# Longer landing times and queue holds for four kinds of loads in a kernel's own instruction planner: pooled attention and a gated MLP, fp32

## The chip, the cores and the metric

The kernel runs on one core of one Trainium2 chip. The metric is the device time of one execution in microseconds (us), lower is better. The engines are TensorE (PE; PEld is its weight load), VectorE (DVE), ScalarE (ACT), GpSimd (POOL), and the queue of SyncE (SP), which issues nearly all DMAs.

## The reference

Attention over pooled keys and values, then an MLP with a GELU of sigmoid form over all 4608 tokens (8 batches of 576), in fp32:

```python
q, k, v: (8, 8, 576, 64)                     # batch, heads, sequence, head width
k_p, v_p = mean over 8 successive positions  # 72 pooled keys and values
attn = softmax(q @ k_p^T / 8) @ v_p
x = attn, heads side by side                 # (4608, 512)
h = x @ w_in                                 # 512 -> 2048
out = (h * sigmoid(1.702 h)) @ w_out         # 2048 -> 512
```

## The kernel before

**The work.** Every fp32 product is made of three products of split operands (a rounded part and the rest): high by high, high by low, low by high. Batches 0 and 1 go through the MLP in the plain way (`dense`, L1208 to L1210 and L1250 to L1252). From batch 2 on the first product of the MLP is made in pairs of hidden blocks by a scheme with seven block products in place of eight (`pair`, products on L1412 into two banks of PSUM that the profile names `ha` and `hb`). It needs sums of blocks of the weights, which `fold` forms once (`stage`, L1295 to L1323), stores to DRAM (`wd`), and which `fetch_pair` loads again for each chunk (`ws` and `shared`, L1345, 512 and 256 KB each). A chunk is 512 tokens of one batch; its eight pairs follow each other on PE, with the second MLP product (`o`, L1613 to L1615) of the pair before between them. A ninth chunk takes the 64 tokens left over in each batch.

**The attention of batch b runs under the MLP of the batches before it.** For b from 2 on its steps are these. The keys come in two loads (`kv_False`, u = 0 and 1), the values in two (`kv_True`), the last eight pooled positions in two (`tl`), each by `fetch_main` and `fetch_tail` on SP; q comes in eight loads (`qr`, two pieces of the sequence by four pairs of heads), each of four DMAs, by `fetch_q`. There is one buffer for `kv` loads after the first batch, one for `tl` and two for `qr`, so a load also waits for the reader of the one before it. DVE sums the eight positions of each pool (`red_k` and `red_v`, L544, about 2 us; `tred`, L605, about 1 us), spreads the sums over block diagonals (`kbd`, `vbd`, L554; `tbd`, L615), and transposes q (`qt`, L731). PE transposes the keys (`kps`), makes the scores (`sps`, L747); DVE and ACT make the softmax (`nm`, `sc`, `sm`), PE the weighted values (`pav`, L949 to L952). What comes out is split and combined for the seven-product scheme (`combine`, L1013 and L1019, tiles `x`, `xs`, `xt`).

**Inside a pair** PE writes seven products into `ha` and `hb`. Between two products into `ha`, `keep` must have copied the bank to SBUF (L1427, ACT or DVE). `plus` (L1434, DVE) adds `hb` to what was kept. ACT then makes the GELU twice (L1451, L1459), POOL or DVE the low part (L1466), and the result feeds the `o` products of the next pair's time. ACT and DVE each take their instructions strictly in the order of the list. A `plus` that comes late therefore holds ACT at the GELU, and a `keep` that stands behind it on ACT holds PE.

**The order of everything** is a list that the kernel works out before it emits a single instruction (class `Plan`). Each step is a task with an engine, an estimated duration and a due time; `order` runs the tasks in a model and emits them in the order in which the model started them. A DMA occupies one modelled queue for its bytes over a rate (340 GB/s for long runs, 80 GB/s for the 128-byte runs of q), and its reader becomes ready 2.2 us after that (`wait`, L126 to L136). So in the list before the change a reader stands no earlier than this after the last DMA of its load began: keys and values 262,144 B / 340 GB/s + 2.2 = 2.97 us; `tl` 65,536 B / 340 GB/s + 2.2 = 2.39 us; q 32,768 B / 80 GB/s + 2.2 = 2.61 us. A table of hand-set shifts of due times (`SHIFTS`) names steps of batches 0 to 2 for the most part; its entries are the same before and after. Nothing in the list changes at run time: each engine executes its part in order and waits on semaphores where the data is not there.

Of the kernel before, what the change touches and what calls it, by code (L numbers as in the profile page):

```python
# [26 lines left out]
WARM = 222.0  # L27
SLACK = 1.5
BLOCKED = 20.0

# [33 lines left out]


class Task:
    __slots__ = "engine us emit due after before bufs ready left begun table k port other mode kind".split()


class Plan:
# [3 lines left out]
    def __init__(self):  # L76
        self.tasks, self.due, self.start = [], 0.0, 0.0

    def add(self, engine, us, emit, reads=(), writes=(), due=None, table=None, also=(), port=False, other=None, mode=None):


        t = Task()
        t.engine, t.us, t.emit, t.table, t.port, t.other = engine, us, emit, table, port, other
        t.due = self.due if due is None else due
        t.mode = mode
        names = [(b[0] if isinstance(b, tuple) else b).name for b in (*writes, *reads)]
        what, number = re.match("([a-z]*)(.*)", names[0]).groups()
        if what in ("raw", "e", "w"):
            number = ""
        else:  # L90
            halves = [n for name in names for n in re.findall("[0-9]_[0-9]+", name)]
            number = (halves or [number])[0]
        t.kind = f"{engine} {what}{number}"
        t.k = len(self.tasks)
        t.before, t.after = set(), []
        t.bufs = []
        for group, is_write in ((reads, False), (writes, True)):
            for b in group:
                b, key = b if isinstance(b, tuple) else (b, None)
                if b not in t.bufs:  # L100
                    t.bufs.append(b)
                    b.users += 1
                for other, k2 in b.writes + (b.reads if is_write else []):
                    if (key is None or k2 is None or key == k2) and not (
                        is_write and engine == other.engine == "DMA" and (other, k2) in b.writes
                    ):
                        t.before.add(other)
                (b.writes if is_write else b.reads).append((t, key))
        for b in also:
            if b not in t.bufs:  # L110
                t.bufs.append(b)
                b.users += 1
        t.before.discard(t)
        for o in t.before:
            o.after.append(t)
        t.left, t.ready, t.begun = len(t.before), self.start, None
        self.tasks.append(t)
        return t
# [8 lines left out]
    @staticmethod  # L127
    def wait(a, b):

        if a.engine == b.engine and a.engine != "DMA":  # L130
            return 0.0
        if a.engine == "DMA" or b.engine == "OUT":
            return 2.2
        if b.engine == "PE":
            return 0.25 if b.due < 150 else 1.2
        return 0.2  # L136
# [15 lines left out]
    def order(self):  # L152
# [33 lines left out]
        while len(placed) < len(self.tasks) or running:  # L186
# [13 lines left out]
            for e in ENGINES:  # L200
# [5 lines left out]
                for t in ready[e]:  # L206
                    if t.ready > now + 1e-9 or e != t.engine and now < t.due:
                        continue
                    rank = (t.due + (BLOCKED if blocked and t.port and e == "DVE" else 0.0), t.k)
                    if (best is None or rank < best[0]) and self.room(t, wanted):  # L210
# [46 lines left out]
def attention_moe_kernel(ctx: ExitStack, tc: tile.TileContext, q, k, v, w_in, w_out, out):  # L257
# [41 lines left out]
    plan = Plan()  # L299
    rings = {}  # L300

    def buf(pool, shape, dtype, tag, name, bufs=None, fifo=False):
        n = bufs or {"xpool": 2, "moe": 2, "ps_o": 4, "ps_h": 2, "ps_a": 2}.get(pool.name, 1)
        ring = rings.setdefault((pool.name, tag), Ring(n, fifo))
        kw = {"bufs": bufs} if bufs else {}
        return Buf(ring, lambda: pool.tile(shape, dtype, tag=tag, name=name, **kw), name)

    def dma(nbytes, emit, reads=(), writes=(), due=None, run=2048):

        us = nbytes / 1e3 / (340.0 if run >= 1024 else 190.0 if run >= 256 else 80.0)  # L310
        return plan.add("DMA", us, emit, reads, writes, due)

    def act(n, emit, reads, writes, table=None, due=None):
        return plan.add("ACT", 0.17 + n * 0.85e-3, emit, reads, writes, due, table)
# [128 lines left out]
    class Part:  # L443
# [8 lines left out]
        @property  # L452
        def ref(self):
            return (self.of, self.key)
# [4 lines left out]
    def fetch_main(b, u, src, t=None):  # L459

        if t is None:
            t = buf(load, [P, NP, 512], F32, "kv", f"kv{b}_{u}_{src is v}", fifo=True)
        for a in range(2):
            dma(
                KM * NP * 2048,
                lambda a=a: nc.sync.dma_start(
                    out=t()[a * KM : (a + 1) * KM],
                    in_=src[b, UH * u + a : UH * (u + 1) : 2, 0 : KM * POOL].rearrange(
                        "j (p w) d -> p j (w d)", w=POOL
                    ),  # L470
                ),
                writes=[ref(t)],
            )
        return t

    def fetch_tail(b, u):

        tl = buf(load, [P, 512], F32, "tl", f"tl{b}_{u}", fifo=True)
        for r, src in enumerate((v, v, v, k)):
            dma(  # L480
                TAIL * 2048,
                lambda r=r, src=src: nc.sync.dma_start(
                    out=tl()[r * TAIL : (r + 1) * TAIL],
                    in_=src[b, UH * u : UH * (u + 1), KM * POOL :].rearrange("h (p w) d -> h p (w d)", w=POOL),
                ),
                writes=[ref(tl)],
            )
        return tl

    def fetch_last(b, part=None):  # L490

        tl = part or buf(load, [P, 512], F32, "tl", f"tl{b}", fifo=True)
        for r, src in enumerate((v, k)):
            dma(
                KM * 2048,
                lambda r=r, src=src: nc.sync.dma_start(
                    out=tl()[r * KM : (r + 1) * KM].rearrange("p (h d) -> p h d", h=H),
                    in_=src[b, :, KM * POOL :].rearrange("h s d -> s h d"),
                ),
                writes=[ref(tl)],  # L500
                run=256,
            )
        return tl

    def fetch_q(b, piece, j):

        o0, tiles = PIECES[piece]
        npc = sum(m for _, m in tiles)
        qr = buf(load, [P, PMAX // 32, 32], F32, "qr", f"qr{b}_{piece}_{j}", bufs=2, fifo=True)
        for a in range(2):  # L510
            for e in range(2):
                r = (2 * a + e) * 32
                dma(
                    32 * npc * 4,
                    lambda r=r, a=a, e=e: nc.sync.dma_start(
                        out=qr()[r : r + 32, 0 : npc // 32],
                        in_=q[b, 2 * j + a, o0 : o0 + npc, e * 32 : (e + 1) * 32].rearrange("(c i) d -> i c d", i=32),
                    ),
                    writes=[qr],
                    run=128,  # L520
                )
        return qr

# [44 lines left out]
    def sum_keys(b, m):  # L568
# [3 lines left out]
        if b < TURNED:  # L572
            tl = m.tl or fetch_last(b)
        for u in range(NU):
            raw = m.k[u] if m.k else fetch_main(b, u, k)
            if b >= TURNED:
                tl = fetch_tail(b, u)
# [87 lines left out]
    def sum_values(b, m):  # L665
        m.vbd = buf(att, [P, NJ, 2, D], F32, "bd", f"vbd{b}", fifo=True)
        for u in range(NU):
            raw = m.v[u] if m.v else fetch_main(b, u, v)
            spread(b, raw, m.vbd, u, f"v{u}")
# [32 lines left out]
    def scores(b, piece, m, whole_q=None):  # L702
# [9 lines left out]
        for j in range(NJ):  # L712
            qt = buf(att, [P, PMAX], F32, "qt", f"qt{n}_{j}", bufs=2)
            if whole_q:
                qps = buf(ps_o, [P, DM], F32, "o", f"qps{n}_{j}")

                def turn(j=j, qps=qps):
                    for (s0, ns), src in zip(tiles, whole_q):
                        nc.tensor.transpose(
                            qps()[:, s0 - o0 : s0 - o0 + ns],  # L720
                            src()[:, 2 * j : 2 * j + 2].rearrange("p h d -> p (h d)"),
                            ident[:ns, :ns],
                        )

                pe(112 * len(tiles), turn, [ref(s) for s in whole_q], [qps], also=[qt])
                copy(npc, lambda copy, qt=qt, qps=qps: copy(out=qt()[:, :npc], in_=qps()[:, :npc]), [qps], [qt])
            else:
                qr = fetch_q(b, piece, j)
                dve(
                    npc,  # L730
                    lambda qt=qt, qr=qr: nc.vector.transpose(  # L731
                        qt()[:, :npc], qr().rearrange("p c d -> p (c d)")[:, :npc]
                    ),
                    [qr],
                    [qt],
                )
# [847 lines left out]
    def begins(c):  # L1584
        return FIRST + STEP * (NF + LAG) + ROUND * (c - 1)
# [41 lines left out]
    for c in range(FROM, B + 1):  # L1627
        acc = {}
        for p in range(NPAIR):
            due = begins(c) + ROUND * p / NPAIR  # L1630
# [45 lines left out]
```

## Time and profile before

| what | value |
|---|---|
| median of 3 runs | 944.16 us (943.03 to 945.93) |
| the profiled execution, its own time | 946.76 us |
| its span, first to last instruction | 944.9 us |
| PE busy in the span | 913.2 us (97%) |
| DVE, ACT, POOL busy | 661.0, 549.2, 311.5 us |
| mean granted TensorE clock | 0.994 |
| DMA moved | 176.71 MB, mean 187 GB/s |

The profile is of one execution, which took 1.86 us more than its span and 2.60 us more than the median of the runs. An engine's idle time is given with what ended it. PEclk is the granted TensorE clock as a share of full speed. A chain of waits goes back from the last instruction to what released each step. In the names, `tred<-tl` is the step that writes `tred` and reads `tl`; the numbers of batches and buffers are left out in the profile. In the rows of the instruction order further down they are kept: `tred7_1` belongs to batch 7, second half of the heads, and the last number only counts buffers.

### The profile page before, as it was taken

To read this page: it belongs to the slowest core of one execution; us is meant where nothing else is said; L and a number is where in the kernel's file an instruction comes from. 1 tells how busy PE (TensorE), PEld (TensorE's weight loads), DVE (VectorE), ACT (ScalarE), POOL (GpSimd) and SP (SyncE) were. 2 spreads that over 40 slices of the span, in tenths; PEclk is the share of its full clock that TensorE was granted. 3 is DMA by queue.
4 is the path that set the end of the run, shared out by engine and by line. 5 is a ranking of instruction groups with operands and counts; after the bars stand their busy time and mean duration, and the time that the engine had idled before them with its cause. 6 is when DMAs were issued, how large, how long until landed. Compare 5 with 4: busy or idle time off the path is not lost.

```text
span 944.9 us, 16303 instructions
## 1 busy us (share of the span) xinstructions
PE 913.2 (97%) x5689; PEld 814.7 (86%) x5689; DVE 661.0 (70%) x1236; ACT 549.2 (58%) x1218; POOL 311.5 (33%) x295
## 2 busy tenths in 40 slices
PE   9999999999899999999999999999899999999997
PEld 9888898888688989898789888988798999899986
DVE  5989878986787777888588867886688642223222
ACT  3778755444448665776467736774477564445443
POOL 1668731878233214225122432233122460000000
PEclk9999999999999999999999999999899999999999
DMA  9994423546647478845884588458764666557541
GB/s 255 376 373 126 122 68 102 155 127 222 187 116 209 135 202 232 235 139 172 250 235 143 182 226 254 152 156 241 213 191 145 206 194 209 164 176 230 178 136 45
DMA packets 145265, 176.71 MB, mean 187 GB/s; under 512 B 85664, under 2 KB 96928, under 8 KB 145184
## 3 DMA queue, kind: packets, MB, share of 16 engines
q1 hardware_dynamic: 140336, 166.89, 59.7%
q10 hardware_dynamic: 4848, 8.78, 2.6%
q8 instruction: 45, 0.74, 0.3%
q14 instruction: 36, 0.29, 0.1%
HBM read 150.47 MB, written 25.17 MB: 186 GB/s over the span
## 4 chain that ended last, share of the span: by engine, by line
PE 71%; DMA 12%; DVE 6%; SPq 6%; ACT 2%; issue 2%; POOL 0%; ACTq 0%; DVEq 0%; POOLq 0%
PE ha L1412 14%; PE hb L1412 11%; PE o L1615 9%; PE o L1614 9%; PE o L1613 9%; DMA qr<-in_q_dram 3%; DMA raw<-in_moe_w_out_dram 3%; PE sps L747 3%; PE h L1208 2%; PE h L1210 2%; PE h L1209 2%; PE o L1251 2%; PE o L1250 2%; PE o L1252 2%; DMA out_dram<-osb 2%
## 5 line engine op out<-in xcount | busy, mean ns | idle before, releaser
L1615 PE MATMUL o<-w,glall 128*128 128x512 f32 x448 | 176.7, 394 | 0.0
L1613 PE MATMUL o<-w,ghall 128*128 128x512 f32 x448 | 176.7, 394 | 0.0
L1614 PE MATMUL o<-w,ghall 128*128 128x512 f32 x448 | 176.1, 393 | 0.0
L1466 POOL TENSOR_TENSOR glall<-shared,ghall 128x256 fp32r<-128x256 f32 x84 | 71.0, 848 | 210.2 <-ACT shared L1459 160.9
L1412 PE MATMUL hb<-x,ws 128*128 128x256 f32 x672 | 99.6, 284 | 4.9 <-DVE shared L1434 3.6
L1412 PEld LDWEIGHTS hb<-x,ws 128*128 128x128 f32 x672 | 91.4, 189 | 13.5 <-DVE shared L1434 7.0
L1412 PEld LDWEIGHTS ha<-xs,ws 128*128 128x128 f32 x672 | 93.3, 189 | 8.4 <-DVE shared L1427 1.6
L1615 PEld LDWEIGHTS o<-w,glall 128*128 128x128 f32 x448 | 84.4, 188 | 18.5
L1412 PE MATMUL ha<-xs,ws 128*128 128x256 f32 x672 | 98.7, 283 | 0.7 <-DVE shared L1427 0.7
L1451 ACT ACTIVATE ghall<-shared 128x256 fp32r<-128x256 f32 x150 | 62.5, 417 | 54.9 <-DVE shared L1434 35.4
L1613 PEld LDWEIGHTS o<-w,ghall 128*128 128x128 f32 x448 | 84.8, 189 | 7.7
L1614 PEld LDWEIGHTS o<-w,ghall 128*128 128x128 f32 x448 | 84.3, 188 | 7.8
L1427 ACT COPY shared<-ha 128x256 f32<-128x256 f32 x116 | 43.0, 371 | 79.5 <-PE ha L1412 73.5
L1466 DVE TENSOR_TENSOR glall<-shared,ghall 128x256 fp32r<-128x256 f32 x66 | 33.1, 502 | 67.4 <-ACT shared L1459 64.9
L1466 POOL TENSOR_TENSOR glall<-gall,ghall 128x256 fp32r<-128x256 f32 x44 | 38.3, 874 | 107.1 <-ACT gall L1459 82.7
L1434 DVE TENSOR_TENSOR shared<-shared,hb 128x256 f32<-128x256 f32 x112 | 46.4, 414 | 38.5 <-PE hb L1412 29.7
L1459 ACT ACTIVATE shared<-shared 128x256 f32<-128x256 f32 x150 | 62.7, 418 | 4.8
L1208 PE MATMUL h<-x,w 128*128 128x256 f32 (+1 forms) x192 | 63.7, 332 | 0.0
L1209 PE MATMUL h<-x,w 128*128 128x256 f32 (+1 forms) x192 | 61.9, 322 | 0.3 <-DVE w L1143 0.3
L1210 PE MATMUL h<-x,w 128*128 128x256 f32 (+1 forms) x192 | 61.7, 321 | 0.0
L1412 PEld LDWEIGHTS ha<-x,shared 128*128 128x128 f32 x336 | 47.4, 191 | 12.6 <-ACT shared L1427 5.0
L1412 PE MATMUL ha<-x,shared 128*128 128x256 f32 x336 | 50.0, 285 | 6.4 <-ACT shared L1427 4.1
(175 smaller groups left out, 2099.9 us busy)
## 6 DMA issues: line engine op xcount, KB each, us to landing
ws<-wd SPq DMA_DIRECT2D x168, 512.0 KB
shared<-wd SPq DMA_DIRECT2D x56, 256.0 KB
out_dram<-osb ACTq DMA_DIRECT2D x32, 256.0 KB
wd<-stage SPq DMA_DIRECT2D x16, 512.0 KB
raw<-in_moe_w_in_dram SPq DMA_DIRECT2D x15, 512.0 KB
raw<-in_moe_w_out_dram SPq DMA_DIRECT2D x15, 512.0 KB
kv_False<-in_k_dram SPq DMA_DIRECT2D x28, 256.0 KB
kv_True<-in_v_dram SPq DMA_DIRECT2D x28, 256.0 KB
```

The costliest lines, as they stand in the source:

```text
L1208: nc.tensor.matmul(o, lhsT=w[:, 0, j], rhs=xs[:, 0], start=j == 0, stop=False)
L1209: nc.tensor.matmul(o, lhsT=w[:, 1, j], rhs=xs[:, 0], start=False, stop=False)
L1210: nc.tensor.matmul(o, lhsT=w[:, 0, j], rhs=xs[:, 1], start=False, stop=j == NJ - 1)
L1412: nc.tensor.matmul(o, lhsT=wv()[:, r, jj], rhs=xo(k, jj), start=start and n == 0, stop=n == len(terms) - 1,  skip_group_check=not start,)
L1427: t = copy(256, lambda copy: copy(out=part(i), in_=bank()[:, 0:256]), [bank], [at(i)])
L1434: lambda: nc.vector.tensor_tensor(out=part(i), in0=part(i), in1=hb()[:, half * 256 : half * 256 + 256], op=ALU.add),
L1451: lambda: nc.scalar.activation(out=gh(), in_=src(), func=AF.Gelu_apprx_sigmoid),
L1459: lambda: nc.scalar.activation(out=part(i), in_=src(), func=AF.Gelu_apprx_sigmoid),
L1466: engine.tensor_tensor(out=gl(), in0=part(i), in1=gh().bitcast(F32), op=ALU.subtract)
L1613: nc.tensor.matmul(o(), lhsT=gh()[:, tok], rhs=w()[:, 0], start=start, stop=False)
L1614: nc.tensor.matmul(o(), lhsT=gh()[:, tok], rhs=w()[:, 1], start=False, stop=False)
L1615: nc.tensor.matmul(o(), lhsT=gl()[:, tok], rhs=w()[:, 0], start=False, stop=stop)
```

## The change

Three kinds of load get a landing time of their own in the list (`LAGS`): keys and values 3.2 us in place of 2.2 (not in batch 0), `tl` 3.0, q 2.5. A DMA now also holds the modelled queue for at least 0.4 us, for `tl` at least 0.7 and for q at least 0.5. With both, the least distance from the start of the last DMA of a load to its reader becomes 0.77 + 3.2 = 3.97 us for keys and values, 0.7 + 3.0 = 3.7 us for `tl`, and 0.5 + 2.5 = 3.0 us for q. No step is added or removed and no operand changes; only the order changes, and for some copies and subtractions the choice between two engines.

```diff
+LAGS = {"kv": 3.2, "tl": 3.0, "qr": 2.5}
...
-    def add(self, engine, us, emit, reads=(), writes=(), due=None, table=None, also=(), port=False, other=None, mode=None):
+    def add(self, engine, us, emit, reads=(), writes=(), due=None, table=None, also=(), port=False, other=None, mode=None, lag=2.2):
...
-        t.mode = mode
+        t.mode, t.lag = mode, lag
...
-        if a.engine == "DMA" or b.engine == "OUT":
+        if a.engine == "DMA":
+            return a.lag
+        if b.engine == "OUT":
             return 2.2
...
-    def dma(nbytes, emit, reads=(), writes=(), due=None, run=2048):
+    def dma(nbytes, emit, reads=(), writes=(), due=None, run=2048, issue=0.4, lag=2.2):
-        us = nbytes / 1e3 / (340.0 if run >= 1024 else 190.0 if run >= 256 else 80.0)
-        return plan.add("DMA", us, emit, reads, writes, due)
+        us = max(issue, nbytes / 1e3 / (340.0 if run >= 1024 else 190.0 if run >= 256 else 80.0))
+        return plan.add("DMA", us, emit, reads, writes, due, lag=lag)
...
     def fetch_main(b, u, src, t=None):
+                lag=LAGS["kv"] if b else 2.2,
     def fetch_tail(b, u):
+                issue=0.7,
+                lag=LAGS["tl"],
     def fetch_q(b, piece, j):
+                    issue=0.5,
+                    lag=LAGS["qr"],
```

The order is the same up to the key sums of batch 1, and differs from there on. Three places matter below. Line numbers after the change are up to 9 higher than before (L1434 is L1443, L605 is L614, L466 is L470).

First place, DVE, before, while the chunk of batch 5 ends and the loads of batch 7 are read. `red7_k1` and `tred7_1` read the second keys and the second `tl` of batch 7; the rows with `hb5_6` and `hb5_7` are `plus` of chunk 5's last two pairs:

```order
L1466 TENSOR_TENSOR glall0_3104<-shared12_3020,ghall0_3096 128x256
L1434 TENSOR_TENSOR shared12_3020<-shared12_3020,hb5_6_7388 128x256
L544 TENSOR_REDUCE red7_k1_7509<-kv7_1_False_7459 128x128
L554 TENSOR_TENSOR kbd7_7453<-red7_k1_7509,mask2_84 128x256
L605 TENSOR_REDUCE tred7_1_7545<-tl7_1_7491 128x64
L1434 TENSOR_TENSOR gall_3155<-gall_3155,hb5_7_7512 128x256
L615 TENSOR_TENSOR tbd7_7479<-tred7_1_7545,mask4_86 128x256
```

The same place on DVE after the change:

```order
L553 TENSOR_REDUCE red7_k1_7453<-kv7_1_False_7384 128x128
L989 TENSOR_TENSOR xs6_3_7414<-pav6_1_3_7440,xs6_3_7414 128x256
L1443 TENSOR_TENSOR shared12_3019<-shared12_3019,hb5_6_7325 128x256
L563 TENSOR_TENSOR kbd7_7389<-red7_k1_7453,mask2_84 128x256
L1028 CAST xs6_2_7501<-xt6_1_7332 128x512
L1022 TENSOR_TENSOR xt6_0_6932<-xt6_0_6932,xt6_1_7332 128x512
L1443 TENSOR_TENSOR gall_3186<-gall_3186,hb5_7_7494 128x256
L1022 TENSOR_TENSOR xs6_4_7516<-xt6_1_7332,xs6_4_7516 128x512
L1475 TENSOR_TENSOR glall0_3140<-gall_3186,ghall0_3128 128x256
L1443 TENSOR_TENSOR shared12_3019<-shared12_3019,hb5_7_7494 128x256
L614 TENSOR_REDUCE tred7_1_7573<-tl7_1_7448 128x64
```

`tred7_1` stood two rows behind `red7_k1`, ahead of the first `plus` of pair 7; now it stands ten rows behind, after two of that pair's `plus`, with part of batch 6's combining between.

Second place, SP, before: the loads of batch 2's first keys, `tl` and q:

```order
L466 DMA kv2_0_False_1783<-in_k_dram 64x2x512 x2
L482 DMA tl2_0_1799<-in_v_dram 32x1x512 x3
L482 DMA tl2_0_1799<-in_k_dram 32x1x512
L515 DMA qr2_0_2_1860<-in_q_dram 32x8x32 x4
L515 DMA qr2_0_3_1882<-in_q_dram 32x8x32 x4
L466 DMA kv2_1_False_1900<-in_k_dram 64x2x512 x2
```

The same place on SP after the change:

```order
L470 DMA kv2_0_False_1786<-in_k_dram 64x2x512 x2
L487 DMA tl2_0_1815<-in_v_dram 32x1x512 x2
L522 DMA qr2_0_2_1833<-in_q_dram 32x8x32 x4
L522 DMA qr2_0_3_1858<-in_q_dram 32x8x32 x4
L487 DMA tl2_0_1815<-in_v_dram 32x1x512
L487 DMA tl2_0_1815<-in_k_dram 32x1x512
L470 DMA kv2_1_False_1901<-in_k_dram 64x2x512 x2
```

The last two DMAs of batch 2's first `tl` are now issued behind eight q DMAs.

Third place, DVE, before: the second values of batch 5 (`red5_v1`), under the first pair of chunk 4 (`hb4_0`); batches 4 and 6 read the same:

```order
L731 STREAM_TRANSPOSE qt5_0_3_5415<-qr5_0_3_5248 128x256
L1434 TENSOR_TENSOR shared12_3020<-shared12_3020,hb4_0_5333 128x256
L544 TENSOR_REDUCE red5_v1_5424<-kv5_1_True_5359 128x128
L554 TENSOR_TENSOR vbd5_5351<-red5_v1_5424,mask2_84 128x256
L770 TENSOR_REDUCE nm5_0_5392<-sps5_0_2_5441 128x2x2
```

The same step on DVE after the change:

```order
L1443 TENSOR_TENSOR gall_3186<-gall_3186,hb4_0_5326 128x256
L740 STREAM_TRANSPOSE qt5_1_0_5482<-qr5_1_0_5386 128x320
L1436 COPY shared12_3019<-ha4_1_5466 128x256
L553 TENSOR_REDUCE red5_v1_5506<-kv5_1_True_5447 128x128
L1443 TENSOR_TENSOR shared12_3019<-shared12_3019,hb4_1_5485 128x256
L804 TENSOR_REDUCE sm5_0_5528<-sc5_0_5393 128x16
```

`red5_v1` has moved from under the first pair of the chunk to the front of the second pair's first `plus` (`hb4_1`).

More of the change, by code (lines that the diff above doesn't have):

```diff
@@ L68 @@
 class Task:
-    __slots__ = "engine us emit due after before bufs ready left begun table k port other mode kind".split()
+    __slots__ = "engine us emit due after before bufs ready left begun table k port other mode kind lag".split()
 class Plan:
```

## The prediction

> **What bounds the kernel now.** The page's head comes first, then the stretches of the span: loading and the plain MLP (0 to 85 us), batches 1 to 3 and the first paired chunks (85 to 290), the regular part with the attention of batches 4 to 7 (290 to 690), the last chunks (690 to 935), and the end. Columns after the stretch's length: busy us and count of PE, PEld, DVE, ACT, POOL, then granted clock, DMA share, GB/s.
>
> ```profile
> span 944.9 us, 16303 instructions
> PE 913.2 (97%) x5689; PEld 814.7 (86%) x5689; DVE 661.0 (70%) x1236; ACT 549.2 (58%) x1218; POOL 311.5 (33%) x295
> ```
>
> ```profile
> 0.00:85.00 85.00, 79.53 (x569) 72.40 (x570) 67.38 (x113) 56.53 (x109) 43.31 (x42) 1.00 0.87 291
> 85.00:290.00 205.00, 199.52 (x1147) 173.79 (x1146) 166.64 (x246) 108.26 (x201) 114.77 (x95) 0.99 0.49 145
> 290.00:690.00 400.00, 384.75 (x2421) 344.21 (x2420) 315.87 (x632) 251.02 (x584) 116.73 (x125) 0.99 0.69 198
> 690.00:935.00 245.00, 244.51 (x1539) 220.62 (x1538) 108.81 (x242) 131.57 (x322) 36.66 (x34) 1.00 0.56 171
> 935.00:945.00 10.00, 4.88 (x22) 3.67 (x20) 2.30 (x5) 1.79 (x4) 0.00 (x0) 0.94 0.39 105
> ```
>
> PE sets the time. Of its 31.7 us without work, 5.47 lie before 85 us, 5.48 in 85 to 290, 15.25 in 290 to 690, 0.49 in 690 to 935, and 5.12 at the end. Batch 7's last scores and weighted values still run after 690 us, but PE is full there: waits on loads are paid where attention and MLP share DVE and ACT, up to then.
>
> Next, what PE waited for in 290 to 690 (us in total, times, longest), the costliest three, and then what DVE waited for there from the loads:
>
> ```profile
> PE ha L1412 <- ACT shared L1427: 4.7, 4, 3.9
> PE hb L1412 <- DVE shared L1434: 3.6, 3, 1.6
> PE ha L1412 <- ACT gall L1427: 2.5, 3, 1.9
> ```
>
> ```profile
> DVE qt L731 <- DMA qr<-in_q_dram: 13.1, 8, 3.4
> ...
> DVE red_k L544 <- DMA kv_False<-in_k_dram: 6.9, 3, 2.4
> ...
> DVE tred L605 <- DMA qr<-in_q_dram: 6.2, 2, 4.0
> ...
> DVE red_v L544 <- DMA kv_True<-in_v_dram: 5.3, 4, 2.8
> DVE tred L605 <- DMA tl<-in_k_dram: 2.7, 2, 1.9
> ```
>
> PE waits on `keep` and `plus`, never on a load. DVE stands 34.2 us before readers of loads (the two `tred` rows, 8.9 us, are one reader: `tred` reads `tl` alone, and the q DMA that one of them names is only the one that landed last). The chain of waits shows how one becomes the other (start, length, what):
>
> ```profile
> 655.34 6.36 DMA tl<-in_v_dram
> 661.71 1.58 DMA qr<-in_q_dram
> ...
> 664.21 0.42 DVE gall L1434
> ...
> 665.58 0.27 ACT shared L1427
> 665.89 1.65 PE ha L1412 x6
> 667.54 0.43 PE o L1613
> ...
> 668.82 1.28 PE hb L1412 x6
> ...
> 671.17 0.72 PE ha L1412 x6
> ...
> 672.61 0.23 PE o L1613
> ```
>
> `tred` waits for `tl` until 663.3; the `plus` (L1434) behind it on DVE is late; ACT has the GELU of that `plus` ahead of a `keep` (L1427); PE sits 3.9 us and starts `ha` at 665.89. The clock then falls: six products take 1.65 us, not 0.72, an `o` 0.43, not 0.23.
>
> So the path is: load late, DVE waits, `plus` late, ACT late, `keep` late, PE waits. The list does not know these waits; in its model the data had arrived. The change moves the readers back in the list, which is the same as issuing the loads earlier for them.
>
> **The change part by part.** The sum is made against the profiled execution, 946.76 us (its span of 944.9 and 1.86 around it), which lies 2.60 above the median, 944.16.
>
> *Up to 85 us and after 690: nothing.* The order is the same up to batch 1's key sums, and after 690 PE has 0.49 us to give; the end after 935 has no loads of these kinds.
>
> *A: batches 4 to 7.* How late is data when the list thinks it there? The rows of the chain that end in a load's landing say how long one took from the issue:
>
> ```profile
> 91.91 4.57 DMA kv_True<-in_v_dram
> ...
> 367.48 5.56 DMA kv_True<-in_v_dram
> ```
>
> ```profile
> 158.22 4.55 DMA tl<-in_k_dram
> ...
> 254.93 3.56 DMA tl<-in_k_dram
> ...
> 342.13 7.04 DMA tl<-in_k_dram
> ```
>
> ```profile
> 384.15 3.70 DMA qr<-in_q_dram
> ...
> 581.33 3.85 DMA qr<-in_q_dram
> ```
>
> Values: mean 5.07, and the list gave 2.97; missing 2.10 before, 1.10 after (3.97). `tl`: mean 5.05 against 2.39; missing 2.66 before, 1.35 after (3.70). q: five such rows in 384 to 585, of which the first and last stand above, mean 4.26 against 2.61; missing 1.65 before, 1.26 after (3.00). The waits of DVE have that size where they occur: `red_k` 6.9/3 = 2.3, `red_v` 1.3, `tred` 8.9/4 = 2.2, `qt` 1.6. So I scale each: keys and values 12.2 × 1.10/2.10 = 6.4; `tl` 8.9 × 1.35/2.66 = 4.5; q 13.1 × 1.26/1.65 = 10.0. Together 20.9 in place of 34.2, 13.3 less.
>
> PE lost 15.25 us to those 34.2, or 0.45 for each. 13.3 × 0.45 = 5.9, so **−5.9**. Bounds: 0, if the waits only move; −15.25, if PE never waits again. I stay near the middle because the rule that carries one wait into PE (a `plus` next behind it) is not removed.
>
> *B: the slow clock.* Around the longest stall the clock was low; after a stall half as long it was not (window, then PE's first instruction after the stall with its idle time in brackets):
>
> ```profile
> 650.00:675.00 25.00, 21.09 (x122) 18.93 (x121) 13.12 (x22) 8.46 (x22) 3.24 (x4) 0.86 0.76 211
> ```
>
> ```profile
> 550.00:575.00 25.00, 23.09 (x148) 20.58 (x147) 15.26 (x25) 10.12 (x27) 4.00 (x5) 1.00 0.87 240
> ```
>
> ```profile
> 565.53 0.98 PE L1412 MATMUL ha<-x,shared 128*128 128x256 f32 x6 [1.91 <-ACT gall L1427]
> ```
>
> At 665.89 it cost 0.93 on `ha`, 3 × 0.20 on `o`, 0.56 on `hb`: 2.1 us. The order fence of the first place shows the `tred` behind this stall, `tred7_1`, moved from two rows behind `red7_k1` to ten, and from ahead of the first `plus` of pair 7 to behind two of them. If its stall falls below 2 us this goes: **−2.1** (bounds 0 and −2.1). A second row shows a low clock after a shorter stall:
>
> ```profile
> 225.00:250.00 25.00, 22.82 (x104) 18.65 (x103) 14.12 (x18) 8.31 (x19) 13.94 (x12) 0.93 0.66 215
> ```
>
> ```profile
> 242.93 0.39 PE L949 MATMUL pav<-ah,vh 128*128 128x256 f32 x1 [2.18 <-DVE x L980]
> ```
>
> So a stall of 1.9 us left the clock whole and one of 2.18 stands in a window at 0.93; I draw the line at 2. The Trainium skill (TensorE: Matmul & The Clock Gate, What's actually happening) says that the clock halves after at least one idle window of about 3.4 us. By that only the stall of 3.9 lowers it, B stays −2.1 and the slower case below loses its 4.2; the row at 242.93 speaks against the rule.
>
> *C: batches 2 and 3, 85 to 290.* The order is shuffled here too. PE has 5.48 us without work there, little of it from loads. The second place (SP) shows the last two DMAs of batch 2's first `tl` issued behind eight q DMAs, six or so more issues ahead of a reader that has not moved as far. How long SP takes for q is in this row, six issues in 5.77 us with nothing between:
>
> ```profile
> 657.72 5.77 SPq L515 DMA_DIRECT2D qr<-in_q_dram  x6
> ```
>
> At that rate eight take 7.7 us; most of it lies before the reader in the list as well. I take one more short stall, **+1.0**: DVE's mean wait for a load above, 34.2/19 = 1.8, times 0.45, rounded up. Bounds: −5.5 (all idle goes) and +5.5 (as much again).
>
> *D: the attention comes later.* In batches 4 to 7 the scores and weighted values stand later among the pairs, and the combined operands are ready nearer the start of the chunk that needs them. The order still has pairs of MLP between, so nothing: **0**. Without that cover each of four chunks would start with a stall like that at 565.53: 4 × 1.91 = +7.6.
>
> Moved choices between ACT and DVE: the same copies, DVE at 79% of 290 to 690 and ACT at 63%: 0, inside C's bounds.
>
> Sum: −5.9 − 2.1 + 1.0 = −7.0. 946.76 − 7.0 = 939.8 for a profiled execution, 937.2 for the median. The range of this case alone is 930 to 941.
>
> **The rivals.** *Slower: the values of batches 4, 5 and 6 become the stall.* The third place shows `red5_v1` moved from under the first pair to directly ahead of the second pair's first `plus`; batches 4 and 6 read alike. The list now starts it as soon as its modelled 3.97 us are over, so any more landing time goes whole into the `plus`, the GELU and the `keep`. The longest wait of `red_v` before was 2.8. Three of those on PE are +8.4, and two that lower the clock 2 × 2.1 = 4.2 more: −7.0 + 12.6 = +5.6, 952.4 profiled, 949.8 median. It decides where the landing takes over about 5 us, for one us of delay passes unseen; the rows above have 4.57 and 5.56. Against it: `red_v` waited four times before for 5.3 us and PE got over most of them. If the clock held, it would be +1.4, 945.6. Chance 0.22.
>
> *No change: the loads are late because SP issues them late.* Six q DMAs took SP 5.77 us, where the list allowed 0.41 each and now 0.5; loads also wait for the reader of their buffer. If lateness comes from the queue, readers moved back drag the next load's buffer back with them, and the waits move along: 0, 944.2. For it: that row, and landings of 7.04 and 6.36 us in the chain, which no fixed lag covers. Against it: the waits of DVE have the size of the missing lag. The Trainium skill (DMA: Bandwidth & Descriptors, Anatomy of one DMA — SWDGE (gpsimd) path) fits about 2.0 us and the bytes at 436 GB/s for one DMA of GpSimd's path, some 2.6 us by my estimate for 256 KB, by which the old list had time enough and A would be 0; the measured landings of 4.57 to 7.04 us speak against it. Chance 0.14.
>
> *A greater gain.* A wait under about a microsecond dies in the slack between `plus` and the next `keep`. If that holds for all that is left, the 15.25 and the 2.1 go: −17.3, 929.5 profiled, 926.9 median. Against it: PE's `hb` waits on DVE are short ones, three for 3.6. Chance 0.10.
>
> **How the numbers follow.** The forecast has 0.54. About 0.3%, 2.8 us, is what a measurement of this kernel can tell from no change, so faster begins below 941.3 and slower above 947.0. Faster: 0.54 + 0.10 = 0.64; within: 0.14; slower: 0.22. Half of the slower case lies above 949.8 and half of the greatest gain below 926.9, 0.16 together; so the range goes from 927 to 950.
>
> **What would show it.** Right: DVE's waits for loads in 290 to 690 near 21 us, in place of 34, `red_k` and `tred` under 1.5 each; no wait of 4 at the last `tred`; PE idle there near 9; the clock of the window around the last `tred` at 1.00; SP's issues as long as before. A is wrong if DVE's waits fall and PE's idle time does not, or if they stay at 34. B is wrong if the clock stays low without such a stall. C is wrong if PE's idle time of 85 to 290 moves by over 3 us. D is wrong if PE waits for `x`, `xs` or `xt` at a chunk's first products. The slower case shows as `red_v` waits of 2.8 and more in batches 4 to 6, with `plus` late behind each.

## The result, and the profile after

The changed kernel takes 933.67 us (median of 4 runs, 930.27 to 934.83), the one before 943.60 in the runs beside it (942.65 to 945.93). The ratio is 0.9885, 95% interval 0.9852 to 0.9918, or 7.7 to 14.0 us less. The forecast was 7.0 us less and 937.2. Two of the medians further down, 931.98 and 939.29, contain one slow execution each (1804.66 and 992.8 us); without it they are 931.45 and 938.83, and the ratios leave it out.

The profiled execution of after took 930.27 us. Its head and its stretches, with the columns of the prediction; the last two stretches are cut where the shorter span ends:

```profile
span 928.2 us, 16289 instructions
PE 908.7 (98%) x5689; PEld 813.3 (88%) x5689; DVE 657.4 (71%) x1232; ACT 545.5 (59%) x1211; POOL 318.8 (34%) x306
```

```profile
0.00:85.00 85.00, 79.56 (x568) 72.94 (x569) 67.07 (x111) 56.25 (x109) 43.34 (x42) 1.00 0.87 291
85.00:290.00 205.00, 201.63 (x1165) 175.18 (x1165) 170.88 (x260) 109.34 (x206) 120.81 (x102) 1.00 0.51 149
290.00:690.00 400.00, 394.52 (x2513) 355.72 (x2513) 317.31 (x640) 263.69 (x620) 121.67 (x133) 1.00 0.70 203
690.00:920.00 230.00, 229.77 (x1435) 207.23 (x1434) 100.33 (x221) 115.25 (x277) 33.02 (x30) 1.00 0.54 170
920.00:928.30 8.30, 3.18 (x14) 2.25 (x13) 1.81 (x3) 0.96 (x2) 0.00 (x0) 0.97 0.48 126
```

PE's time without work, as length less busy time:

| stretch | before | after |
|---|---|---|
| 0 to 85 | 5.47 | 5.44 |
| 85 to 290 | 5.48 | 3.37 |
| 290 to 690 | 15.25 | 5.48 |
| 690 to the end's stretch (935 before, 920 after) | 0.49 | 0.23 |
| the end | 5.12 | 5.12 |

The span is 16.7 us shorter: 12.2 us of it is idle time of PE, 9.8 in the regular part, and 4.5 is busy time of PE (913.2 to 908.7), which the clock explains for the most part, as shown below. That is more than the 9.9 us between the medians, because each profile shows one execution: before's lies 3.2 us above its median, after's 3.4 below.

What PE waited for in 290 to 690, and DVE's waits there that a load ended:

```profile
PE ha L1421 <- DVE shared L1436: 1.8, 3, 0.9
PE hb L1421 <- DVE gall L1443: 1.4, 2, 1.2
PE ha L1421 <- DVE gall L1436: 0.9, 1, 0.9
PE ha L1421 <- ACT shared L1436: 0.8, 1, 0.8
PE hb L1421 <- DVE shared L1443: 0.3, 1, 0.3
```

```profile
DVE red_v L553 <- DMA kv_True<-in_v_dram: 8.1, 5, 2.7
...
DVE qt L740 <- DMA qr<-in_q_dram: 4.0, 5, 1.2
DVE red_k L553 <- DMA kv_False<-in_k_dram: 3.3, 2, 2.2
...
DVE tred L614 <- DMA qr<-in_q_dram: 2.1, 2, 1.1
...
DVE tred L614 <- DMA kv_False<-in_k_dram: 0.3, 1, 0.3
```

No stall of PE is longer than 1.2 us there. DVE's waits went from 34.2 to 17.8 us, very unevenly: the transposes of q from 13.1 to 4.0, `tred` from 8.9 to 2.4, keys and values only from 12.2 to 11.4, with `red_v` up from 5.3 to 8.1. The two windows of low clock are whole again:

```profile
225.00:250.00 25.00, 24.66 (x124) 20.38 (x123) 16.94 (x25) 9.68 (x22) 12.23 (x12) 1.00 0.66 213
650.00:675.00 25.00, 25.00 (x163) 22.77 (x162) 18.54 (x36) 15.10 (x32) 3.42 (x5) 1.00 0.93 271
```

### The profile page after: what moved, and what is told of

The parts are those of the page before. It is cut to its first block, busy times and chain, and to the rows that moved or that the text cites. A ratio compares the mean times of both kernels' runs of the same rounds, so it can differ in the third digit from the quotient of the medians.

```text
span 928.2 us, 16289 instructions
## 1 busy us (share of the span) xinstructions
PE 908.7 (98%) x5689; PEld 813.3 (88%) x5689; DVE 657.4 (71%) x1232; ACT 545.5 (59%) x1211; POOL 318.8 (34%) x306
## 4 chain that ended last, share of the span: by engine, by line
PE 76%; DMA 8%; DVE 7%; SPq 3%; ACT 2%; issue 2%; ACTq 0%; DVEq 0%
PE ha L1421 14%; PE hb L1421 11%; PE o L1624 9%; PE o L1623 9%; PE o L1622 9%; PE sps L756 3%; DMA raw<-in_moe_w_out_dram 3%; PE h L1217 3%; PE h L1219 3%; PE h L1218 3%; PE o L1260 2%; PE o L1259 2%; PE o L1261 2%; DMA ws<-wd 2%; DMA kv_True<-in_v_dram 1%
## 5 line engine op out<-in xcount | busy, mean ns | idle before, releaser
L1475 POOL TENSOR_TENSOR glall<-shared,ghall 128x256 fp32r<-128x256 f32 x91 | 74.5, 819 | 233.9 <-ACT shared L1468 176.1
L1443 DVE TENSOR_TENSOR shared<-shared,hb 128x256 f32<-128x256 f32 x112 | 46.4, 414 | 54.6 <-PE hb L1421 36.6
L1436 ACT COPY shared<-ha 128x256 f32<-128x256 f32 x103 | 38.2, 371 | 73.0 <-PE ha L1421 71.2
L1475 DVE TENSOR_TENSOR glall<-shared,ghall 128x256 fp32r<-128x256 f32 x59 | 29.8, 505 | 41.8 <-ACT shared L1468 40.4
L1475 POOL TENSOR_TENSOR glall<-gall,ghall 128x256 fp32r<-128x256 f32 x37 | 29.9, 810 | 83.4 <-ACT gall L1468 62.8
L1421 PE MATMUL ha<-x,ws 128*128 128x256 f32 x336 | 51.0, 287 | 3.7 <-DVE shared L1436 1.8
L1247 POOL TENSOR_TENSOR gl<-g,gh 128x512 fp32r<-128x512 f32 x27 | 36.4, 1349 | 52.1 <-ACT gh L1239 50.3
```

The costliest lines, as they stand in the source:

```text
L1421: nc.tensor.matmul(o, lhsT=wv()[:, r, jj], rhs=xo(k, jj), start=start and n == 0, stop=n == len(terms) - 1,  skip_group_check=not start,)
L1436: t = copy(256, lambda copy: copy(out=part(i), in_=bank()[:, 0:256]), [bank], [at(i)])
L1443: lambda: nc.vector.tensor_tensor(out=part(i), in0=part(i), in1=hb()[:, half * 256 : half * 256 + 256], op=ALU.add),
L1475: engine.tensor_tensor(out=gl(), in0=part(i), in1=gh().bitcast(F32), op=ALU.subtract)
```

## The experiments

The theory: the change pays because it moves readers to where their loads have landed, so that DVE waits less and PE with it. The rival that grew out of the result: the order of before is an unlucky draw, and any other arrangement of the list is better, whatever it allows for landing. All medians below stand beside 943.9 to 944.0 us for before in the same runs.

**The price of all waits for loads.** The same edit in both orders:

```diff
-in_=raw().rearrange("p i (w d) -> p i d w", w=POOL)
+in_=homes[1, 3]().bitcast(F32).rearrange("p i (w d) -> p i d w", w=POOL)
...
-in_=tl().rearrange("p (w d) -> p d w", w=POOL)
+in_=homes[1, 3]().bitcast(F32)[:, 0].rearrange("p (w d) -> p d w", w=POOL)
...
-qr().rearrange("p c d -> p (c d)")[:, :npc]
+(homes[1, 3]().bitcast(F32)[:, 0] if b >= TURNED else qr().rearrange("p c d -> p (c d)"))[:, :npc]
```

> The order of before, instruction for instruction, with one thing changed: from batch 2 on the sums of keys, values and tl and the transposes of q read a resident block of w_out in place of the loaded tile (the loads are still made, but nothing waits for them, and the attention is that of other data). It gives the price of all waits for loads in the order of before. Theory (these waits are what the change takes away): DVE's 34 us of waits for loads in 290 to 690 go, PE's idle time there falls from 15 us to 3 to 6, the low clock goes, and the time comes out 10 to 15 us below before, 929 to 934. Rival (the new order is better of itself, the waits cost little): 939 to 943.

> The same edit in the order of after: from batch 2 on no reader waits for a load (it reads a resident block of w_out, so the attention is that of other data). Theory: 1 to 5 us below after, 929 to 932, and within 3 us of the same edit in the order of before, since without waits both orders are equally good. Rival (a better order of itself): as much below after as the other is below before, so some 8 to 10 us below the same edit in the order of before, 924 or less.

Measured: 930.80 us in the order of before (ratio 0.9859, 0.9827 to 0.9891) and 924.84 in the order of after (0.9807, 0.9777 to 0.9837). The regular stretch, first in the order of before, then of after:

```profile
290.00:690.00 400.00, 393.31 (x2497) 354.95 (x2496) 327.71 (x660) 261.03 (x612) 120.08 (x131) 1.00 0.70 203
```

```profile
290.00:690.00 400.00, 398.20 (x2548) 360.46 (x2547) 323.01 (x651) 266.05 (x628) 125.13 (x134) 1.00 0.72 206
```

Waits for loads cost before 13.1 us, as the theory has it, and after still 8.8. (The idle time of PE, 6.7 us, is a little above the 3 to 6 that were expected in the order of before, and its window of 650 to 675 is at 0.93, so the low clock did not go everywhere.) But the two orders are not equally good without them: 6.0 us lie between, of which PE's idle time in this stretch is 6.69 − 1.80 = 4.9. So of the change's 10 us some 4 are cheaper waits, and 6 are an order that is better of itself: both theories hold in part. The largest stall that is left in the order of before has another cause. In that kernel's rows ACT copies a block of the output, issues its store (`out_dram`) 2.3 us after that copy has ended, then runs the `keep`, and PE waits for it:

```profile
564.21 0.59 ACT L1163 COPY osb<-o 128x512 f32<-128x512 f32 x1 [1.49 <-DMA out_dram<-osb]
...
567.13 0.34 ACTq L1164 DMA_DIRECT2D out_dram<-osb  x1
567.57 0.37 ACT L1427 COPY shared<-ha 128x256 f32<-128x256 f32 x1 [2.77 <-DMA qr<-in_q_dram]
```

```profile
568.00 0.39 PE L1412 MATMUL ha<-x,ws 128*128 128x256 f32 x1 [2.28 <-ACT shared L1427]
```

ACT ran nothing for 2.77 us before the `keep`, and nothing was issued on it in that time but the store; that the store held the `keep` is read from this order. In this edit loads also no longer wait for a reader to free their buffer, so the price is that of both.

**Where it happens.** The change for batches 4 to 7 alone (below), and for 0 to 3 alone (the same with `b < 4`, and the first line left at 0.4). The hold of 0.4 us binds for no load but `tl`, which has its own, since the bytes of all others hold the queue longer:

```diff
-    def dma(nbytes, emit, reads=(), writes=(), due=None, run=2048, issue=0.4, lag=2.2):
+    def dma(nbytes, emit, reads=(), writes=(), due=None, run=2048, issue=0.0, lag=2.2):
...
-                lag=LAGS["kv"] if b else 2.2,
+                issue=0.4 if b >= 4 else 0.0,
+                lag=LAGS["kv"] if b >= 4 and b else 2.2,
...
-                issue=0.7,
-                lag=LAGS["tl"],
+                issue=0.7 if b >= 4 else 0.0,
+                lag=LAGS["tl"] if b >= 4 else 2.2,
...
-                    issue=0.5,
-                    lag=LAGS["qr"],
+                    issue=0.5 if b >= 4 else 0.0,
+                    lag=LAGS["qr"] if b >= 4 else 2.2,
```

> The change for the loads of batches 4 to 7 alone: holds and landing times as before for batches 0 to 3, whose order stays that of before. Theory (A and B of the prediction carry the gain): 934 to 937, with PE's idle time in 290 to 690 at 5 to 7 us. Rival (the gain comes from the rearranged part before 290 us): 940 to 944.

> The complement: the change for the loads of batches 0 to 3 alone, those of 4 to 7 as before. Theory: 940 to 943, waits for loads in 290 to 690 of 25 us or more on DVE and 10 us or more of idle time on PE there. Rival: 934 to 937.

Measured: 931.98 us (0.9879, 0.9848 to 0.9911) and 932.05 (0.9873, 0.9841 to 0.9906). Each half alone brings the whole gain. The first goes past the theory's expectation a little; the second refutes it as it was put, since the loads of batches 4 to 7 have their old landing times there. The regular stretch of the second, and DVE's waits for loads in it:

```profile
290.00:690.00 400.00, 392.83 (x2494) 353.49 (x2493) 319.37 (x652) 257.36 (x602) 125.83 (x131) 1.00 0.70 203
```

```profile
DVE tred L615 <- DMA tl<-in_k_dram: 12.5, 4, 4.8
DVE qt L741 <- DMA qr<-in_q_dram: 6.7, 6, 1.4
DVE red_v L554 <- DMA kv_True<-in_v_dram: 1.1, 1, 1.1
DVE red_k L554 <- DMA kv_False<-in_k_dram: 1.0, 1, 1.0
```

With the same allowance the waits are 21.3 us in place of 34.2, and PE idles 7.2 us in place of 15.25. The list behind batch 3 came out otherwise; that its readers stand better by chance is likely and not shown.

**Is nearly any other order better?** Two controls, both without holds: 2.1 us, then 2.3, for batches 4 to 7 (the edit above with `issue=0.0` and these numbers in `LAGS`).

> Control: no holds, and a landing time of 2.1 us in place of 2.2 for the loads of batches 4 to 7. PE's order is that of before throughout, only DVE, ACT and SP are arranged a little otherwise. Theory (what counts is the landing time that the list allows): as before or a little worse, 942 to 948, 30 us or more of waits for loads on DVE in 290 to 690. Rival (the order of before is an unlucky draw, and nearly any rearrangement of batches 4 to 7 takes its costly stall away, as the run with batches 0 to 3 alone suggests): 930 to 937.

> A second control on the other side: 2.3 us for the loads of batches 4 to 7, no holds; 53 of PE's 3116 places differ from before. Theory: a tenth of the way, 940 to 945. Rival (unlucky draw): 930 to 937.

Measured: 944.41 us (1.0002, 0.9987 to 1.0017) and 945.57 (1.0019, 1.0000 to 1.0037). The first has 29.2 us of waits where 30 or more were expected, the second lies just above its range. Both keep a stall of 3.2 us of the kind that the prediction followed. But they are hardly other draws: in DVE's rows, put side by side without the numbers of batches, the first differs from before at no more than 5 places and the second at no more than 10, against 79 and 94 in the two runs above and 69 and 100 in two that follow (940.63 and 941.99 us). So the two controls show that a list which keeps the stalls keeps the time, and they do not test the rival. The wider rearrangements do: they bring from 2 to 12 us, and one with less landing time below loses 19. That nearly any other order brings the whole gain is refuted by this; that the order of before is a poor one of itself is not, and the 6 us above speak for it.

**The parts.** From batch 4 on: the landing times without holds, the holds without landing times, and the change without the landing time of keys and values.

```diff
-LAGS = {"kv": 3.2, "tl": 3.0, "qr": 2.5}
+LAGS = {"kv": 2.2, "tl": 3.0, "qr": 2.5}
```

> The landing times of the change (3.2, 3.0, 2.5) for batches 4 to 7, without any hold of the queue; 91 of PE's places differ from before. Theory: most of the gain, 932 to 937, DVE's waits for loads in 290 to 690 at 22 us or less. If the holds carry it: 939 to 944.

> The holds of the queue alone (0.7 for tl, 0.5 for q) for batches 4 to 7, landing times at 2.2. Theory: a small part, 938 to 943, since the holds add 0.5 us to tl and 0.1 to q of the 1.5 and 0.4 that the change adds. If the holds carry it: 932 to 936. Unlucky draw: 930 to 937 here too.

> The run of the change from batch 4 on (931.98), but with the landing time of keys and values left at 2.2 us (hold 0.77 by bytes); tl and q as in the change. After the change DVE still waits 11.4 us for keys and values, before 12.2, so their term in the prediction earned little. If it earns nothing: 930 to 934. If it is worth its share of A, 12.2 of 34.2: 934 to 939.

Measured: landing times alone 941.80 us (0.9978, 0.9957 to 0.9998), holds alone 940.63 (0.9970, 0.9950 to 0.9990), both without keys and values 941.99 (0.9978, 0.9958 to 0.9997). The theory had expected most of the gain of the landing times alone (932 to 937), and the last run lies above both of its ranges. Taken singly the parts bring 2 to 3 us, together 12. DVE's waits add up nearly (27.3 and 21.5 us against 34.2, and 15.1 with both), the time does not. The landing time of keys and values is worth 10 us here, four times what the prediction gave it (5.8 us of waits by 0.45, 2.6 us). With it DVE waits 6.5 us for keys and values, and 16.6 without it:

```profile
DVE red_v L554 <- DMA kv_True<-in_v_dram: 9.3, 4, 2.8
DVE red_k L554 <- DMA kv_False<-in_k_dram: 7.3, 4, 2.5
DVE qt L741 <- DMA qr<-in_q_dram: 6.8, 7, 2.9
DVE qt L741 <- DMA ws<-wd: 0.8, 1, 0.8
```

`red_k` waits 7.3 us here and not at all with it. But the landing times alone, with the same 3.2 us for keys and values, leave 13.8 us of these waits: it is the list that all the numbers make together, and not this one by itself.

**Less and more.** Landing times of 1.2 from batch 4 on without holds; then 4.6, 4.4 and 3.5 with holds, from batch 4 on and everywhere (`LAGS` alone, so keys and values not in batch 0).

> The other way: 1.2 us of landing time in place of 2.2 for the loads of batches 4 to 7, no holds, batches 0 to 3 as before. Theory: the lag that is missing grows from 2.1, 2.7 and 1.7 us to 3.1, 3.7 and 2.7; DVE's waits in 290 to 690 grow from 34 to some 50 us, PE loses 0.45 of that, 948 to 956. Rival (the time follows the order by chance, not the landing time): 938 to 946.

> More of the same from batch 4 on: 4.6 us for keys and values, 4.4 for tl, 3.5 for q, holds as in the change; with the holds the list then gives 5.4, 5.1 and 4.0 us, as much as the landings that the trace showed. Theory: DVE's waits for loads under 8 us in 290 to 690, PE's idle time there 2 to 4, 928 to 932. Rival (the attention now comes so late that the chunks wait for x, xs and xt): 934 or more, with PE waits for these at the chunks' first products.

> The same larger landing times for all batches but the first, a candidate for a better kernel. Theory: below the change's 933.67, 925 to 931, near the 924.84 of the run in which no reader waits. Rival (later attention costs as much as the waits did): 934 to 940.

Measured: 962.60 us with less (1.0204, 1.0181 to 1.0228), the right way and twice as far as the middle of what was expected, though DVE's waits grew to 41.5 us and not to some 50. With more 939.29 from batch 4 on (0.9945, 0.9925 to 0.9964) and 935.13 everywhere (0.9910, 0.9890 to 0.9931): the theory's numbers fail, and the rival's ranges (934 or more, 934 to 940) hold. DVE's waits fell as the theory said, if not quite as far from batch 4 on (10.9 us, where under 8 were expected). The regular stretch with less, then with more everywhere:

```profile
290.00:690.00 400.00, 376.11 (x2331) 338.21 (x2330) 293.36 (x601) 244.87 (x576) 113.71 (x121) 0.97 0.66 188
```

```profile
290.00:690.00 400.00, 392.10 (x2496) 353.55 (x2495) 321.08 (x634) 267.30 (x628) 119.70 (x127) 1.00 0.71 202
```

With more everywhere DVE waits 3.0 us for loads, and PE still idles 7.9. The rival's mechanism fails too: PE waits for no `x`, `xs` or `xt` at a chunk's start. In the run from batch 4 on its longest stall comes from the stores again (ACT, then DVE, then PE):

```profile
473.66 0.57 ACT L1173 COPY osb<-o 128x512 f32<-128x512 f32 x1
477.13 0.34 ACTq L1174 DMA_DIRECT2D out_dram<-osb  x1
477.56 0.59 ACT L1173 COPY osb<-o 128x512 f32<-128x512 f32 x1 [3.34 <-DMA out_dram<-osb]
```

```profile
479.85 0.42 DVE L1476 TENSOR_TENSOR glall<-gall,ghall 128x256 fp32r<-128x256 f32 x1 [4.90 <-ACT gall L1469]
...
481.91 1.89 DVE L554 TENSOR_REDUCE red_v<-kv_True 128x128 f32<-128x1024 f32 x1
483.72 0.41 DVE L1437 COPY shared<-ha 128x256 f32<-128x256 f32 x1
```

```profile
484.18 0.51 PE L1422 MATMUL ha<-xs,ws 128*128 128x256 f32 x2 [2.96 <-DVE shared L1437]
```

A store is issued 2.9 us after its copy ended, the next one and the GELU behind it are late, DVE stands 4.9 us, and then has scores and a `red_v` to do ahead of the `keep`. The sum had no wait of this kind.

All runs in one table, by DVE's waits for loads in 290 to 690 (waits and idle time from one execution each):

| run | DVE waits | PE idle there | median |
|---|---|---|---|
| 1.2 us from batch 4 | 41.5 | 23.9 | 962.60 |
| before | 34.2 | 15.3 | 943.9 |
| 2.1 us from batch 4 | 29.2 | 11.6 | 944.41 |
| 2.3 us from batch 4 | 28.1 | 14.6 | 945.57 |
| landing times alone | 27.3 | 11.7 | 941.80 |
| without keys and values | 24.2 | 11.7 | 941.99 |
| holds alone | 21.5 | 10.4 | 940.63 |
| batches 0 to 3 alone | 21.3 | 7.2 | 932.05 |
| after | 17.8 | 5.5 | 933.67 |
| batches 4 to 7 alone | 15.1 | 4.4 | 931.98 |
| more, from batch 4 | 10.9 | 7.3 | 939.29 |
| more, all | 3.0 | 7.9 | 935.13 |
| no waits, order of before | 0 | 6.7 | 930.80 |
| no waits, order of after | 0 | 1.8 | 924.84 |

Down to about 18 us of waits, PE's idle time falls with them, by some 0.78 us for each (23.9 − 5.5 over 41.5 − 17.8). Below that it doesn't: 2 to 8 us, by the order. These are different lists, so the 0.78 is not the price of a wait alone. Within one order that price is smaller: taking all waits for loads away lowers PE's idle time from 15.25 to 6.69 us in the order of before, 0.25 for each of the 34.2, and from 5.48 to 1.80 in that of after, 0.21 for each of the 17.8. No version that waits for its loads is clearly faster than after: the two halves lie 1.7 and 1.6 us below it, inside the intervals.

## Why the prediction was right

The sign, the place and the chain of causes held: 933.67 lies inside 927 to 950, though 3.5 us below the forecast, and the main case was the one that came. That the forecast came so near is partly luck: the price of a wait was too high, the gain of the new order of itself was not in the sum, and C had the wrong sign. The sizes below are those of two single executions, 16.5 us apart where the medians are 9.9 apart; which terms the other 6.6 belong to is not known.

- **A, batches 4 to 7, mis-sized.** Forecast −5.9, in the profiles −9.8. DVE's waits came out near the forecast (17.8 for 20.9), but the step that failed is "PE lost 15.25 us to those 34.2, or 0.45 for each". Without any wait for a load PE still idles 6.69 us in the order of before, so the loads had caused 8.6 of the 15.25, or 0.25 for each; by that the 13.3 us that the prediction took away are worth 3.3. Of the 9.8, waits for loads gave 4.9 (8.6 before, 3.7 after), and 4.9 is the order of itself (6.69 to 1.80), for which the sum had no term. Nor is the price the same everywhere: the row of batch 5 below shows a wait of 2.7 us that cost PE nothing. The split by kind failed as well: keys and values were to fall to 6.4 and stayed at 11.4, q to 10.0 and fell to 4.0. One kind's landing time moves the readers of the others, so the terms are no sum; `red_k`, which was to wait under 1.5 us, still waits up to 2.2.
- **B, the clock, right.** Forecast −2.1; the windows around the last `tred` (at 648.9) are at 1.00, and that wait of 4.0 is gone: `tred` waits at most 1.1 us.
- **C, batches 2 and 3, wrong in sign and inside its bounds.** Forecast +1.0, in the profiles −2.1 of idle time. A short stall came, but not for a load of batch 2's `tl`: at 92.32 PE waits 1.9 us for `raw`, a block of the weights that DVE makes ready (row below). The one of 2.18 at 242.93 went, and the low clock behind it with it. The sign is the order's own: PE idles 3.3 to 3.4 us in 85 to 290 in all three traces with the new order there, and 4.8 to 8.1 in the nine with the old one that wait for loads. The products `h` (before, then after; busy us, mean ns, then idle time) took 187.3 us in all before and 185.5 after: 1.8 us that the sum did not have. With B's 2.1 this is most of the 4.5 us of PE's busy time. In half of the traces with the old order the clock stays whole at this place (last section), so these 1.8 are in part the luck of the profiled execution.

```profile
L1208 PE MATMUL h<-x,w 128*128 128x256 f32 (+1 forms) x192 | 63.7, 332 | 0.0
L1209 PE MATMUL h<-x,w 128*128 128x256 f32 (+1 forms) x192 | 61.9, 322 | 0.3 <-DVE w L1143 0.3
L1210 PE MATMUL h<-x,w 128*128 128x256 f32 (+1 forms) x192 | 61.7, 321 | 0.0
```

```profile
L1217 PE MATMUL h<-x,w 128*128 128x256 f32 (+1 forms) x192 | 63.2, 329 | 2.0 <-DVE raw L1131 1.9 <-ACT gh L1239 0.2
L1218 PE MATMUL h<-x,w 128*128 128x256 f32 (+1 forms) x192 | 61.2, 319 | 0.3 <-DVE w L1152 0.3
L1219 PE MATMUL h<-x,w 128*128 128x256 f32 (+1 forms) x192 | 61.1, 318 | 0.0
```

- **D, later attention, right** so far as it goes: PE waits for no `x`, `xs` or `xt` at a chunk's first products, even with landing times nearly half as long again.
- **The slower rival came as a wait, but not as a price.** DVE did wait for `red_v` in batches 4, 5 and 6: 2.2, 2.7 and 1.7 us, close to the 2.8 it assumed. Here is batch 5:

```profile
474.43 0.39 DVE L1436 COPY shared<-ha 128x256 f32<-128x256 f32 x1
477.48 2.01 DVE L553 TENSOR_REDUCE red_v<-kv_True 128x128 f32<-128x1024 f32 x1 [2.66 <-DMA kv_True<-in_v_dram]
479.40 0.41 DVE L1443 TENSOR_TENSOR shared<-shared,hb 128x256 f32<-128x256 f32 x1
```

The `plus` starts 2.5 us after the products into `hb` ended (476.85), and PE has no wait at all between 470 and 486. The `keep` of that pair stands ahead of the wait on DVE, so PE had what it needed; the rival's price took the wait for the stall.
- **No change** fell: the waits did not move along, though SP still issues q in bursts, six in 3.33 us in this row of after:

```profile
654.87 3.33 SPq L522 DMA_DIRECT2D qr<-in_q_dram  x6
```

- **The greater gain** fell for its premise: with 3.0 us of waits left, PE still idles 7.9 us, on stores and on the order.

What stays open: which feature of the order makes 6.7 us of PE's idle time without any load in one list and 1.8 in the other (the stores explain 2.3 of it by one row), and why the halves and the whole end at the same time. The stores were not tried by themselves.

## What to carry to other kernels

In a list made by a planner a wrong landing time shows as waits of the readers' engine, and the experiment that prices it is to let the readers read something resident, in both orders: it says how much is to be had, and how much of a gain is only another order. The longest allowance is not the best: here a landing time of 1.2 us cost 19 us, and allowances as long as the landings in the chain (5.4, 5.1 and 4.0 us in place of the change's 3.97, 3.7 and 3.0) gave back 7 us in one list, and 1.5, inside the intervals, in the other. Don't add up terms by kind of load, and don't lay all idle time to the waits that you see, nor price a wait by an average: look at what stands behind it.

## What the runs showed of the hardware

The low clock after a short idle time comes and goes. Ten traces have the order of before up to 290 us and the same stall of 2.2 us, which ends between 241.0 and 244.4 us; in five the window 225 to 250 is at 0.93, in five at 1.00. Here is the same place in two executions, with more landing time from batch 4 on and with the change from batch 4 on, whose orders agree there:

```profile
242.68 0.39 PE L959 MATMUL pav<-ah,vh 128*128 128x256 f32 x1 [2.20 <-DVE x L990]
...
243.29 0.63 PE L1218 MATMUL h<-x,w 128*128 128x512 f32 x1
...
245.85 0.63 PE L1218 MATMUL h<-x,w 128*128 128x512 f32 x1
246.28 0.55 PE L1219 MATMUL h<-x,w 128*128 128x512 f32 x1
```

```profile
242.73 0.39 PE L959 MATMUL pav<-ah,vh 128*128 128x256 f32 x1 [2.19 <-DVE x L990]
...
243.31 0.42 PE L1218 MATMUL h<-x,w 128*128 128x512 f32 x1
...
245.43 0.40 PE L1218 MATMUL h<-x,w 128*128 128x512 f32 x1
```

In the first, the products run at 0.63 us in place of 0.40 from 243.3 to 246.3, some 3 us. The prediction's line at 2 us is therefore no threshold. The Trainium skill (TensorE: Matmul & The Clock Gate, What's actually happening) says that the observed window runs free, which fits that the same stall falls on either side; the length of about 3.4 us that it gives for an idle window is more than the 2.2 us that these traces show as enough.

A DMA that ACT issues can hold ACT by 2 to 3 us after the copy that it waits for has ended, in rows above at 567.13 and 477.13. SP was issuing two DMAs of q in part of that time, from 563.70 to 565.85 and from 475.58 to 477.78 us; whether that is the cause wasn't tried.
